# A fused memory attention and feed-forward kernel: padded token rows, keys loaded first, and small matmuls issued in fixed bundles

## The chip, the cores and the metric

The kernel runs on one core of a Trainium2 chip. The metric is the device time of one execution in microseconds (us); the median of three runs is used. TensorE does the matmuls, VectorE and ScalarE the elementwise work, GpSimd small copies, and SyncE issues all DMA transfers.

## What is computed

Eight batches of 576 tokens, eight heads of 64, 32 memory slots per head, then a feed-forward layer of 2048 on the 512 joined columns:

```python
a = phi - np.max(phi, axis=2, keepdims=True)          # over the tokens
a = np.exp(a); a = a / (np.sum(a, axis=2, keepdims=True) + 1e-09)
k_m = np.einsum('bhsm,bhsd->bhmd', a, k)              # 32 x 64 per head
v_m = np.einsum('bhsm,bhsd->bhmd', a, v)
scores = scale * np.matmul(q, k_m.transpose(0, 1, 3, 2))
attn = softmax(scores)                                # over 32 slots
x = np.matmul(attn, v_m)                              # heads joined: 4608 x 512
h = x @ w_in                                          # 512 x 2048
sp = np.maximum(h, 0.0) + np.log1p(np.exp(-np.abs(h)))
out = (h * erf(sp)) @ w_out                           # 2048 x 512
```

The kernel never forms x. It multiplies v_m with w_in once per batch (called "value products" here, `vw`) and multiplies attn with that.

## The kernel before

The weights arrive as 64-bit words and are decoded to float32 on the chip (`decode`: per block of 1 MB, three passes on VectorE and two on ScalarE). Most operands are then split into a high and a low part in float32r, and a product is made of three such matmuls; the first four steps of the first layer and the first sixteen of the second use plain float32 instead, which TensorE runs as two passes (two rows in the trace for one matmul in the program).

A step is one block of 128 hidden columns for the 576 tokens of one batch: sixteen steps to a batch, 128 in all. For a step `ffn1` (L681) makes h in two halves of 288 tokens, VectorE copies it from PSUM (L696), ScalarE runs softplus (L704) and erf (L709) for four steps at a time because each of the two needs its own table, VectorE forms and splits g, and `ffn2` (L754) multiplies by w_out into four PSUM tiles `pso`, one for each 128 tokens. The last 64 tokens of two batches are collected and multiplied together (`psr`).

For each batch four small kinds of TensorE work come ahead of its steps:
- sums (L540): k_m and v_m, by `one_memory`, for two groups of four heads one after the other. Stationary is a block of phi (128 tokens x 32), moving are K and V of a head side by side (128 columns). Tokens lie in chunks of 128, 128, 128, 128 and 64. 20 program matmuls for a group, 4 of them at a time on four column strips of TensorE.
- two transposes that put k_m and v_m (`kvk`, L557) into the layout that the next two kinds want.
- scores (L583, tiles `q`, `km`): q times k_m for 288 tokens, twice per batch (`attention`). Their softmax is ten steps on VectorE and two on ScalarE; its exponential may run only where a group of four softplus or erf ends.
- value products (L583, tiles `w_in`, `vm`): four per batch from the second batch on, with 512 columns.

Sums use TensorE in strips of 32 columns and 128 rows (64 for the last chunk), scores and value products in strips of 32 columns and 64 rows; everything else uses the whole array. A stretch of such small matmuls between two whole-array matmuls is called a visit below.

The order is made by `Plan`: each operation is recorded with an engine, a cost, a rank (100 times the step at which it is wanted), what it reads and writes and which buffers it needs; `order()` runs through a model of the engines' time and writes one fixed program order for each engine. Among what is ready TensorE takes the lowest rank; once in a visit it goes on with other small work that is ready. PSUM has four tiles `ps`, shared by h, all small work and `psr`. While TensorE has nothing in the head, `fill` puts matmuls on zeros there (`idle`, L365). All loads go through SyncE in that order: `load_kv` and `load_phi` take two DMAs each (512 tokens and the last 64), `load_weight` 1 MB, `load_q` 576 KB. The head's list is `FIRST`.

Of the kernel before, what the change touches and what calls it, by code (L numbers as in the profile page):

```python
# [28 lines left out]
SCRATCH = 1024  # L29

# [39 lines left out]
class Plan:  # L70
# [5 lines left out]
    SWITCH = 92.0  # L76
    RELOAD = 100.0
# [160 lines left out]
def tile_memory_attention_then_erf_softplus_ffn(  # L238
# [13 lines left out]
    H = 2 * kv.shape[1]  # L252
    D = 64
# [12 lines left out]
    SC = [(c * P, min(P, S - c * P)) for c in range((S + P - 1) // P)]  # L266
    RAW = 4
# [10 lines left out]
        for n, b, kw in (  # L278
# [9 lines left out]
            ("ot", 2, {}),  # L288
# [6 lines left out]
    room.update({"g_hi": 3, "g_lo": 3, "raw": RAW, "ot": 2, "ps": 4, "sc": 2, "dk": 1, "phiT": 2})  # L295
    room.update({f"pso{d}": 1 for d in range(NT)})
    for n in ("pmx", "psm", "prs"):
# [10 lines left out]
        "ot": ("ot", [P, DM], F32),  # L308
# [18 lines left out]
    def mm(n, exact):  # L327
        return 2 * (2 * n / 2.4 + 2.5) if exact else n / 2.4 + 11.7
# [10 lines left out]
    zeros = const.tile([P, 512], BF16, name="zeros")  # L339
# [12 lines left out]
    def split(rank, hi, lo, src, n, get_hi, get_lo, get_src, psum=False):  # L352
        op(ACT, on_act(n, psum), rank, [src], [hi],
           lambda: nc.scalar.activation(get_hi(), get_src(), AF.Identity))  # L354
        op(DVE, on_dve(n), rank, [src, hi], [lo],
           lambda: nc.vector.tensor_tensor(  # L356
               out=get_lo(), in0=get_src(), in1=get_hi().bitcast(F32), op=ALU.subtract))
# [3 lines left out]
    def fill(n):  # L361
        if n and not idle:
            idle.append(pools["po"].tile([P, DM], F32, name="idle", tag="pso0"))
        for _ in range(n):
            nc.tensor.matmul(out=idle[0], lhsT=zeros[:, :P], rhs=zeros, start=True, stop=True)  # L365


    def load(rank, key, nbytes, emit):
        op(SP, 60, rank, [], [key], emit, nbytes=nbytes)

    def load_weight(rank, name, c):
        key = tile_("wo", "w", name, c, shape=[P, NP_ * 256], dtype=I64, pool="wo")

        def emit():
            t = get(key)
            if name == "in":
                nc.sync.dma_start(
                    out=t.rearrange("p (r f) -> p r f", r=NP_),
                    in_=w_in[:, :, c * 256 : (c + 1) * 256],
# [6 lines left out]
        load(rank, key, P * 8192, emit)  # L386

    def load_phiT(rank, b, g):
        key = tile_("phiT", "phiT", b, g)
        load(rank, key, P * S * 4,  # L390
             lambda: nc.sync.dma_start(out=get(key), in_=phiT[b, g * P : (g + 1) * P, :]))

    def load_tokens(rank, key, src, n_bytes, view):
        n = S // P
        load(rank, (key, "whole"), S // P * P * n_bytes, lambda: nc.sync.dma_start(
            out=view()[:, :n], in_=src[: n * P].rearrange("(p c) e -> p c e", c=n)))
        load(rank + 0.001, (key, "last"), SC[-1][1] * n_bytes, lambda: nc.sync.dma_start(
            out=view()[: SC[-1][1], n], in_=src[n * P :]))

    def load_phi(rank, b):  # L400
        key = tile_("raw", "phi", b, shape=[P, len(SC), H * M], pool="raw")
        load_tokens(rank, key, phi[b], H * M * 4, lambda: get(key))

    def load_kv(rank, b, p, tag="raw"):
        key = tile_(tag, "kv", b, p, shape=[P, len(SC), 2, 2, D], pool=tag)
        load_tokens(rank, key, kv[b, p], 4 * D * 4,
                    lambda: get(key).rearrange("p c x h d -> p c (x h d)"))

    def load_q(rank, u, tag="raw"):
        key = tile_(tag, "q", u, shape=[P, NP_, U], pool=tag)  # L410
        b, hf = divmod(u, 2)
        load(rank, key, P * NP_ * U * 4, lambda: nc.sync.dma_start(
# [6 lines left out]
    def words(key):  # L419
        v = get(key).bitcast(I32).rearrange("p (n two) -> p n two", two=2)  # L420
        return v[:, :, 0], v[:, :, 1]

    def decode(rank, name, c):
        key = ("w", name, c)
        lo, hi = (key, "lo"), (key, "hi")

        def clamp():
            hf = words(key)[1].bitcast(F32)
# [4 lines left out]
        def low():  # L433
            v = words(key)[0]
            nc.scalar.activation(v, v.bitcast(U32), AF.Identity, scale=LOW)  # L435

        def rebias():
            hf = words(key)[1].bitcast(F32)
            nc.scalar.activation(hf, hf, AF.Identity, scale=REBIAS)  # L439

        def merge():
            v, w = words(key)
# [4 lines left out]
        if name == "in":  # L447
            dst = ("w_in", c)
        elif c < NPR - 1:
# [4 lines left out]
        def sign():  # L454
            v, w = words(key)
            if name == "in":
                to = w_in_sb[c // 2][:, :, c % 2 * 256 : (c % 2 + 1) * 256]
# [489 lines left out]
```

## Time and profile before

| | |
|---|---|
| median of three runs | 731.49 us (730.93 to 731.76) |
| the profiled execution | 729.75 us, span of its instructions 728.0 us |
| TensorE busy | 720.0 us (99%), 4816 matmuls |
| VectorE, ScalarE, GpSimd busy | 521.0 us (72%), 449.9 us (62%), 98.7 us (14%) |
| chain that ended last | TensorE 87%, DMA 6%, ScalarE 4% |
| granted TensorE clock | 0.999 of full speed (the 2.4 GHz level) |

Matmuls are pipelined: the length that a row gives for one is longer than the distance to the next, so the pace of TensorE is read from the distance between starts. TensorE also counts as busy while it multiplies zeros in the head. Page section 2 shows VectorE and ScalarE nearly full in the second to the seventh of forty slices and at five to eight tenths later.

### The profile page before, as it was taken

What the parts mean: (1) busy time and instruction counts of PE and PEld (TensorE: products, weight loads), DVE (VectorE), ACT (ScalarE), POOL (GpSimd) and SP (SyncE); (2) the same over time, 40 slices, a digit from 0 to 9 for tenths busy, and PEclk for the clock granted to TensorE, in tenths of its full rate; (3) what the DMA queues carried; (4) which work ended last, traced back from release to release, by engine and by line L of the source; (5) the groups of instructions that cost most, each with busy time, mean ns of one, the idle gap of its engine ahead of it and who ended that gap; (6) DMA issues with size and microseconds to landing.
All of it is one profiled execution on the core that took longest, in us unless ns stands there. A gap on an engine that the chain in (4) does not pass through costs nothing.

```text
span 728.0 us, 12307 instructions
## 1 busy us (share of the span) xinstructions
PE 720.0 (99%) x4816; PEld 553.8 (76%) x4816; DVE 521.0 (72%) x963; ACT 449.9 (62%) x708; POOL 98.7 (14%) x246
## 2 busy tenths in 40 slices
PE   9999999999999999999999999999999999999997
PEld 4456555578887888888788887888878788888885
DVE  3899999689677685877755587777854587666631
ACT  5799999875747666594644556474754266454611
POOL 0011001120111111111111011111111111111110
PEclk9999999999999999999999999999999999999999
DMA  9996332421503115111310214211210100010002
GB/s 321 391 389 227 100 149 82 161 100 43 173 24 108 42 39 178 35 59 34 107 57 1 91 48 127 70 59 33 66 33 1 59 15 0 1 45 15 1 1 72
DMA packets 30393, 64.75 MB, mean 89 GB/s; under 512 B 2688, under 2 KB 13440, under 8 KB 29312
## 3 DMA queue, kind: packets, MB, share of 16 engines
q1 hardware_dynamic: 30336, 63.97, 26.1%
q8 instruction: 38, 0.62, 0.4%
q14 instruction: 19, 0.16, 0.1%
HBM read 54.53 MB, written 9.44 MB: 88 GB/s over the span
## 4 chain that ended last, share of the span: by engine, by line
PE 87%; DMA 6%; ACT 4%; DVE 1%; SPq 1%; issue 1%
PE pso L754 48%; PE psh L681 26%; PE psr L754 6%; PE psa L583 5%; DMA w<-w_in 4%; PE psa L540 2%; DMA kv<-kv 2%; ACT w L439 1%; ACT w L435 1%; ACT e L709 0%; ACT L709 0%; PE psa L557 0%; ACT e L704 0%; DVE w L443 0%; ACT vw_hi L354 0%
## 5 line engine op out<-in xcount | busy, mean ns | idle before, releaser
L754 PE MATMUL pso<-wo,g_hi 128*128 128x512 f32 x896 | 280.8, 395 | 0.0
L704 ACT ACTIVATE e<-h 128x576 f32<-128x576 f32 x128 | 88.0, 687 | 171.5 <-DVE h L696 170.9
L754 PEld LDWEIGHTS pso<-wo,g_hi 128*128 128x128 f32 x896 | 160.0, 188 | 31.8 <-issue 6.3
L754 PE MATMUL pso<-wo,g_lo 128*128 128x512 f32 x448 | 176.1, 393 | 0.0
L696 DVE COPY h<-psh 128x288 f32<-128x288 f32 x239 | 107.8, 452 | 42.8 <-PE psh L681 41.2
L681 PE MATMUL psh<-at_hi,vw_hi 128*128 128x288 f32 x496 | 113.7, 310 | 0.0
L681 PE MATMUL psh<-at_hi,vw_lo 128*128 128x288 f32 x496 | 106.0, 295 | 0.3 <-DVE vw_lo L356 0.3
L681 PE MATMUL psh<-at_lo,vw_hi 128*128 128x288 f32 x496 | 106.1, 295 | 0.0
L681 PEld LDWEIGHTS psh<-at_hi,vw_hi 128*128 128x128 f32 x496 | 84.5, 188 | 27.8 <-issue 8.2
L735 POOL CAST rest<-g_hi 128x64 fp32r<-128x64 f32 x112 | 51.1, 457 | 391.3 <-DVE g_hi L730 385.5
L728 DVE TENSOR_TENSOR e<-e,h 128x576 f32<-128x576 f32 x112 | 82.7, 751 | 26.5 <-ACT e L709 26.4
L754 PEld LDWEIGHTS pso<-wo,g_lo 128*128 128x128 f32 x448 | 84.1, 188 | 19.2
L730 DVE CAST g_hi<-e 128x576 fp32r<-128x576 f32 x112 | 50.7, 457 | 63.1 <-PE pso L754 51.1
L731 DVE TENSOR_TENSOR g_lo<-e,g_hi 128x576 fp32r<-128x576 f32 x112 | 86.3, 771 | 4.4
L709 ACT ACTIVATE e<-e 128x576 f32<-128x576 f32 x128 | 80.3, 675 | 0.4
L681 PEld LDWEIGHTS psh<-at_hi,vw_lo 128*128 128x128 f32 x496 | 79.8, 188 | 0.7 <-DVE vw_lo L356 0.5
L681 PEld LDWEIGHTS psh<-at_lo,vw_hi 128*128 128x128 f32 x496 | 79.1, 188 | 0.0
L735 POOL CAST rest<-g_lo 128x64 fp32r<-128x64 f32 x112 | 37.8, 338 | 110.8 <-DVE g_lo L731 103.7
L754 PE MATMUL pso<-w,g 128*128 128x512 f32 x112 | 52.5, 599 | 0.0
L754 PE MATMUL psr<-wo,rest 128*128 128x512 f32 x192 | 49.0, 390 | 0.0
L354 ACT ACTIVATE vw_hi<-psa 128x512 fp32r<-128x512 f32 (+1 forms) x68 | 34.9, 556 | 19.6 <-PE psa L583 19.5
L356 DVE TENSOR_TENSOR vw_lo<-psa,vw_hi 128x512 fp32r<-128x512 f32 (+1 forms) x68 | 42.0, 632 | 6.5 <-ACT vw_hi L354 6.3
(82 smaller groups left out, 716.0 us busy)
## 6 DMA issues: line engine op xcount, KB each, us to landing
kv<-kv SPq DMA_DIRECT2D x32, 512.0 KB, 4.2
q<-qT SPq DMA_DIRECT2D x16, 576.0 KB, 5.0
w<-w_in SPq DMA_DIRECT2D x8, 1024.0 KB, 11.6
w<-w_out SPq DMA_DIRECT2D x8, 1024.0 KB, 11.2
out<-ot SPq DMA_DIRECT2D x32, 256.0 KB, 2.0
phiT<-phiT SPq DMA_DIRECT2D x16, 288.0 KB, 2.9
phi<-phi SPq DMA_DIRECT2D x8, 512.0 KB, 5.7
kv<-kv SPq DMA_DIRECT2D x32, 64.0 KB, 4.2
```

The source lines that it names most:

```text
L354: lambda: nc.scalar.activation(get_hi(), get_src(), AF.Identity))
L356: lambda: nc.vector.tensor_tensor(out=get_lo(), in0=get_src(), in1=get_hi().bitcast(F32), op=ALU.subtract))
L583: nc.tensor.matmul(out=get(ps[par])[p * M : (p + 1) * M, :], lhsT=w()[rows, p, :], rhs=x()[rows, p, :], start=True, stop=True,)
L681: nc.tensor.matmul(out=get(ps), lhsT=x[:, g, k % 4 * P : (k % 4 + 1) * P], rhs=y[:, g, :], start=(n + g == 0), stop=(n == len(parts) - 1 a ...
L696: lambda: nc.vector.tensor_copy(out=keep(), in_=get(ps)),
L704: last[:] = [op(ACT, on_act(S), rank, [("h", i)], [e], lambda: nc.scalar.activation(get(e), get(("h", i)), AF.Softplus), kind="softplus", ...
L709: last[:] = [op(ACT, on_act(S), rank, [e], [e], lambda: nc.scalar.activation(get(e), get(e), AF.Erf), kind="erf", edge=edge, after=last)]
L728: op(DVE, on_dve(S), rank, [e, h], [e], lambda: nc.vector.tensor_tensor(out=get(e), in0=get(e), in1=get(h), op=ALU.mult))
L730: op(DVE, on_dve(S, 1), rank, [e], [hi], lambda: nc.vector.tensor_copy(out=get(hi), in_=get(e)))
L731: op(DVE, on_dve(S), rank, [e, hi], [lo], lambda: nc.vector.tensor_tensor(out=get(lo), in0=get(e), in1=get(hi).bitcast(F32), op=ALU.subtract))
L735: lambda x=x, y=y: nc.gpsimd.tensor_copy(out=rest[:, k, x, cols], in_=get(y)[:, NT * P :]))
L754: nc.tensor.matmul(out=o, lhsT=y, rhs=z, start=(start and n == 0), stop=(stop and n == len(parts) - 1))
```

## The change

- K and V come as separate arrays, and all token tables are padded on the host to five chunks of 116 rows (the last 112) in 128 partitions, so that each load is one DMA of 640 KB and every chunk takes more than 64 rows. `Plan`'s costs for a switch of strips and for a 512-column matmul are raised.
- The first batch: the loads come as phiT, K, first half of q, the first block of w_in, V, second half of q. phi itself isn't loaded: the exponential of phiT is transposed instead. Its K memories are made first and its first scores go ahead of V (`EARLY`).
- Sums have 64 moving columns instead of 128, since K and V are apart: 80 program matmuls per batch where there were 40, five chunks each.
- From the second batch on one call makes the sums of both groups (`TOGETHER`); from the third batch on `bundle` joins small work into single operations: sums with the third value product of the batch before, the first scores with its fourth, the second scores with the first value product of the batch itself.
- The rest's low part is made on GpSimd for the first batch (`rest_split` is gone), `ot` tiles live in the slots of `phiT`, and ScalarE copies the final results alone.

```diff
+ROW = 116
-    SWITCH = 92.0
-    RELOAD = 100.0
+    SWITCH = 98.0
+    RELOAD = 170.0
...
-    RAW = 4
+    ROWS = [min(ROW, S - c * ROW) for c in range(NC)]
+    RAW = 5
...
+    def together(rank, *pieces):
+        for x in pieces:
+            next(x)
+        reads, writes, holds, emits, cost = [], [], [], [], 0.0
+        for x in pieces:
+            c, r, w, k, emit = next(x)
+            cost, reads, writes, holds = cost + c, reads + r, writes + w, holds + k
+            emits.append(emit)
+        op(PE, cost, rank, reads, writes, lambda: [f() for f in emits], kind="small", holds=holds)
+        for x in pieces:
+            next(x, None)
...
         def sums():
-            for c, (s0, ln) in enumerate(SC):
-                for j in range(4):
-                    h = 4 * g + j
-                    nc.tensor.matmul(
-                        out=get(ps)[M * j : M * (j + 1), 0, :],
-                        lhsT=get(a)[:ln, c, h * M : (h + 1) * M],
-                        rhs=get(("kv", b, h // 2))[:ln, c, :, h % 2, :],
...
+            for n, g in enumerate(gs):
+                for y, x in enumerate(xs):
+                    for c, ln in enumerate(ROWS):
+                        for j in range(4):
+                            h = 4 * g + j
+                            nc.tensor.matmul(
+                                out=get(ps)[M * j : M * (j + 1), n, y * D : (y + 1) * D],
+                                lhsT=get(a)[:ln, c, h * M : (h + 1) * M],
+                                rhs=get(("kv", b, x, g))[:ln, c, j * D : (j + 1) * D],
...
-    FIRST = ["phiT0", "phiT1", "phi", "kv0", "kv1", "in0", "kv2", "kv3", "q0", "q1", "in1", "out0"]
+    FIRST = ["phiT0", "phiT1", "k0", "k1", "q0", "in0", "v0", "v1", "q1", "in1", "out0"]
...
-        n = o - 12 if b == 1 else max(o - 21, NK - 2)
+        n = o - 8 if b == 1 else max(o - 18, NK - 2)
...
-            n = o - (8 if b == 1 else 11) + 4 * x
+            n = o - 8 + 4 * x if b == 1 else o - 7 + 3 * x
             when(n, load_q, at(n - 4), 2 * b + x)
-            when(n, attention, at(n), at(n + 1), 2 * b + x)
-        for p in range(4):
-            n = o - 3 + 4 * p
-            when(n, vw, at(n), b, 2 * p, 2, False)
+        PARTS = [(o - 8, [(attention, 2 * b)]), (o - 4, [(attention, 2 * b + 1)]), (o - 3, [(vw, b, 0)])]
+        if b > 1:
+            PARTS = [
+                (o - 11, [(one_memory, b, TOGETHER[0]), (vw, b - 1, 8)]),
+                (o - 7, [(attention, 2 * b), (vw, b - 1, 12)]),
+                (o - 4, [(attention, 2 * b + 1), (vw, b, 0)]),
+            ]
+        PARTS.append((o + 1, [(vw, b, 4)]))
+        if b == B - 1:
+            PARTS += [(o + 5, [(vw, b, 8)]), (o + 9, [(vw, b, 12)])]
```

What this does to the order of the instructions, at three places. First TensorE's sums for the last batch. Before, the first group of heads follows a value product:

```order
L754 MATMUL pso<-wo,g_hi 128x512 x2
L754 MATMUL pso<-wo,g_lo 128x512
L583 MATMUL psa<-w_in_103,vm_101 32x512 x8
L540 MATMUL psa<-kv,phi 32x128 x20
L681 MATMUL psh<-at_hi,vw_hi 128x288 x2
L681 MATMUL psh<-at_lo,vw_hi 128x288 x2
```

The second group's twenty stand twenty-four rows further on, in a visit of their own. In the changed kernel, for the same batch:

```order
L796 MATMUL pso<-wo,g_lo 128x512
L796 MATMUL psr<-wo,rest 128x512 x6
L585 MATMUL psa<-kv,phi 32x64 x80
L637 MATMUL psa<-w_in_102,vm_98 32x512 x8
L796 MATMUL pso<-wo,g_hi 128x512 x2
L796 MATMUL pso<-wo,g_lo 128x512
```

Both groups, K and V apart, now stand in one visit, and a value product follows the sums instead of leading them. Second, TensorE's first scores of the last batch. Before they stand alone:

```order
L754 MATMUL pso<-wo,g_hi 128x512 x2
L754 MATMUL pso<-wo,g_lo 128x512
L583 MATMUL psa<-q,km_100 32x288 x8
L754 MATMUL pso<-wo,g_hi 128x512 x2
L754 MATMUL pso<-wo,g_lo 128x512
```

In the changed kernel:

```order
L796 MATMUL pso<-wo,g_hi 128x512 x2
L796 MATMUL pso<-wo,g_lo 128x512
L637 MATMUL psa<-q,km_97 32x288 x8
L637 MATMUL psa<-w_in_103,vm_98 32x512 x8
L796 MATMUL pso<-wo,g_hi 128x512 x2
L796 MATMUL pso<-wo,g_lo 128x512
```

The fourth value product of the seventh batch stands behind them in the same visit. Over the whole program there are 51 visits before and 40 in the changed kernel; behind the visit that holds the last value product of the first batch there are 38 and 29. Third, TensorE's start without the matmuls on zeros, whose rows are left out of both (112 in all before, 78 now). Before:

```order
L501 MATMUL psa<-ident,bias 128x128 x2
...
L540 MATMUL psa<-kv,phi 32x128 x20
...
L557 MATMUL psa<-ident,kvk 128x128 x2
...
L540 MATMUL psa<-kv,phi 32x128 x20
...
L557 MATMUL psa<-ident,kvk 128x128 x2
...
L583 MATMUL psa<-q,km_99 32x288 x16
...
L583 MATMUL psa<-w_in_103,vm_101 32x256 x8
...
L681 MATMUL psh<-at,vw_hi 128x288 x8
```

In the changed kernel:

```order
L557 MATMUL psa<-ident,phiT 112x128
...
L585 MATMUL psa<-kv,phi 32x64 x40
...
L607 MATMUL psa<-ident,kvk 128x128 x2
...
L637 MATMUL psa<-q,km_96 32x288 x8
...
L585 MATMUL psa<-kv,phi 32x64 x40
L637 MATMUL psa<-q,km_96 32x288 x8
L607 MATMUL psa<-ident,kvk 128x128 x2
...
L637 MATMUL psa<-w_in_100,vm_98 32x256 x8
...
L737 MATMUL psh<-at,vw_hi 128x288 x4
...
L637 MATMUL psa<-w_in_100,vm_98 32x256 x8
```

The first scores stand ahead of V's sums, the second behind them, and the first four matmuls of `ffn1` (two steps, first half of the tokens) no longer wait for the second scores.

## Rows read from the trace of the kernel before

**Rows 1.** By stretch: us, each engine's busy us (instructions), clock, DMA share, GB/s
```profile
0.00:30.00 30.00, 28.38 (x222) 12.56 (x223) 16.87 (x34) 16.96 (x34) 0.70 (x6) 1.00 0.98 353
30.00:50.00 20.00, 19.44 (x129) 11.69 (x128) 19.39 (x29) 18.46 (x30) 1.50 (x2) 1.00 1.04 380
...
200.00:300.00 100.00, 100.00 (x693) 81.30 (x692) 72.56 (x146) 63.78 (x99) 15.27 (x38) 1.00 0.25 78
```

**Rows 2.** TensorE in order of time, lone visit: start, length, operation, count
```profile
607.83 0.62 PE L754 MATMUL pso<-wo,g_hi 128*128 128x512 f32 x2
608.28 0.40 PE L754 MATMUL pso<-wo,g_lo 128*128 128x512 f32 x1
608.61 1.09 PE L583 MATMUL psa<-w_in,vm 64*32 64x512 f32 x16
609.63 0.53 PE L681 MATMUL psh<-at_hi,vw_hi 128*128 128x288 f32 x2
610.00 0.42 PE L681 MATMUL psh<-at_lo,vw_hi 128*128 128x288 f32 x2
610.26 0.43 PE L681 MATMUL psh<-at_hi,vw_lo 128*128 128x288 f32 x2
```

**Rows 3.** The same view, value products followed by scores
```profile
499.19 1.09 PE L583 MATMUL psa<-w_in,vm 64*32 64x512 f32 x16
500.07 0.69 PE L583 MATMUL psa<-q,km 64*32 64x288 f32 x16
500.69 0.74 PE L754 MATMUL pso<-wo,g_hi 128*128 128x512 f32 x2
```

**Rows 4.** The same view, value products followed by sums
```profile
518.47 1.09 PE L583 MATMUL psa<-w_in,vm 64*32 64x512 f32 x16
519.49 1.43 PE L540 MATMUL psa<-kv,phi 128*32 128x128 f32 x40
520.85 0.53 PE L681 MATMUL psh<-at_hi,vw_hi 128*128 128x288 f32 x2
```

**Rows 5.** The same view, sums alone
```profile
527.90 1.43 PE L540 MATMUL psa<-kv,phi 128*32 128x128 f32 x40
529.27 0.73 PE L754 MATMUL pso<-wo,g_hi 128*128 128x512 f32 x2
```

**Rows 6.** Stretches of those sums: matmuls (PE) and weight loads (PEld) under way
```profile
527.90:527.96 0.06, 0.06 (x4) 0.06 (x8) 1.00 0.00 0
527.90:528.03 0.13, 0.13 (x4) 0.13 (x8) 1.00 0.00 0
...
527.90:528.72 0.82, 0.82 (x32) 0.81 (x32) 1.00 0.00 0
```

**Rows 7.** TensorE's order of time in the head
```profile
20.19 0.84 PE L583 MATMUL psa<-q,km 64*32 64x288 f32 x16 [0.29 <-DMA q<-qT]
...
22.09 7.73 PE L365 MATMUL idle<-zeros 128*128 128x512 bf16 x35
29.66 4.04 PE L681 MATMUL psh<-at,vw_hi 128*128 128x288 f32 x16
```

**Rows 8.** VectorE's and ScalarE's order of time in the head
```profile
12.82 0.70 DVE L429 TENSOR_SCALAR w<-w 128x1024 f32<-128x1024 f32 x1 [3.99 <-DMA w<-w_in]
...
28.26 1.43 DVE L650 STREAM_TRANSPOSE at<-sc 128x576 f32<-128x576 f32 x2
...
31.31 1.22 DVE L465 SCALAR_TENSOR_TENSOR w_in<-w 128x1024 int32<-128x1024 int32 x1
...
27.96 1.17 ACT L435 ACTIVATE w<-w 128x1024 int32<-128x1024 uint32 x1 [0.58 <-DMA w<-w_in]
```

**Rows 9.** TensorE's order of time at the third batch's sums
```profile
129.16 1.42 PE L540 MATMUL psa<-kv,phi 128*32 128x128 f32 x36 [0.58 <-DMA kv<-kv]
```

**Rows 10.** Groups by line and shape: busy us, mean ns, idle before
```profile
L704 ACT ACT_TABLE_LOAD x33 | 42.3, 1283 | 0.6
...
L521 ACT ACTIVATE phiT<-phiT,pmx 128x576 f32<-128x576 f32 x16 | 12.3, 771 | 0.1
```

More of the change, by code (lines that the diff above doesn't have):

```diff
@@ L265, in tile_memory_attention_then_erf_softplus_ffn @@
     REST = S - NT * P
-    SC = [(c * P, min(P, S - c * P)) for c in range((S + P - 1) // P)]
-    RAW = 4
+    NC = phi.shape[2]
+    ROWS = [min(ROW, S - c * ROW) for c in range(NC)]
+    assert NC == -(-S // ROW) and D < ROWS[-1]
+    RAW = 5
     HB, EB = 5, 5
@@ L364, in fill, with load, load_weight @@
         for _ in range(n):
[L365 to L372, printed above, removed]
+            nc.tensor.matmul(
+                out=idle[0].rearrange("p (n c) -> p n c", c=P), lhsT=zeros,
+                rhs=zeros.unsqueeze(1).to_broadcast([P, DM // P, P]), start=True, stop=True,
+            )
+    def load(rank, nbytes, keys, emit):
+        op(SP, 60, rank, [], keys, emit, nbytes=nbytes)
+    def load_weight(rank, name, c, x=None):
+        n = 256 if x is None else P
+        key = tile_("wo", "w", name, c, x, shape=[P, NP_ * 256], dtype=I64, pool="wo")
         def emit():
@@ new lines, in memories @@
+        if not b:
+            tile_("raw", *a, shape=[P, NC, H * M], pool="raw")
+            n = NC - 1
+            for g in range(NG):
+                numbers_of(rank, b, g, range(n), tile_("ps", "psa", "a", g, shape=[P, n, P], pool="ps"), 0)
+            last = tile_("ps", "psa", "a", NG, shape=[P, NG, P], pool="ps")
+            for g in range(NG):
+                numbers_of(rank, b, g, range(n, NC), last, g)
+        for turn_n, part in enumerate(parts):
+            together(rank_2 + turn_n * 0.01, one_memory(rank_2 + turn_n * 0.01, b, part))
@@ L576, in heads @@
-    def heads(rank, reads, w, x, n, holds, *key):
-        ps = [tile_("ps", "psa", *key, par, shape=[P, n], pool="ps") for par in range(2)]
-        def emit():
-            for p in range(NP_):
-                for par in range(2):
-                    rows = slice(par * D, (par + 1) * D)
-                    nc.tensor.matmul(
-                        out=get(ps[par])[p * M : (p + 1) * M, :],
-                        lhsT=w()[rows, p, :],
-                        rhs=x()[rows, p, :],
-                        start=True,
-                        stop=True,
-                    )
-        op(PE, 4 * n / 2.4, rank, reads, ps, emit, kind="small", holds=holds)
-        return ps
@@ new lines, in heads, with of_heads @@
+    def heads(n, *key):
+        return [tile_("ps", "psa", *key, par, shape=[P, n], pool="ps") for par in range(2)]
+    def of_heads(ps, w, x):
+        for p in range(NP_):
+            for par in range(2):
+                rows = slice(par * D, (par + 1) * D)
+                nc.tensor.matmul(
+                    out=get(ps[par])[p * M : (p + 1) * M, :],
+                    lhsT=w[rows, p, :],
+                    rhs=x[rows, p, :],
+                    start=True,
+                    stop=True,
+                )
@@ L670, in ffn1 @@
         ws = [("vw_hi", b, k // 4)] if exact else [("vw_hi", b, k // 4), ("vw_lo", b, k // 4)]
-        part = [(k // 2 % 2, par) for par in range(2)] if b == 0 else [(0, par) for par in range(2)]
+        part = [(k % 4, par) for par in range(2)]
         h = ("h", i)
@@ L852, in tile_memory_attention_then_erf_softplus_ffn @@
             when(2 * c - 3, decode, at(2 * c - 3), "in", c)
-            when(2 * c - 1, vw, at(2 * c - 1.5), 0, c, 1, 2 * c < FR1)
-        when(2 * c, decode, at(second[2 * c] - 3.5), "out", c)
+            n = at(2 * c - 1.5)
+            when(2 * c - 1, lambda n=n, c=c: together(n, vw(n, 0, 2 * c, 2, 2 * c < FR1)))
+        when(2 * c, decode, at(second[2 * c] - 2.5), "out", c)
         n = second[16 + 2 * c] - 5 - c if 2 * c < FR2 else second[2 * c] - 2
```

311 lines of the change are left out of this document (163 added, 148 removed).

## The prediction

> **What bounds the kernel now.** I read the engines' busy time by stretch first, since the page's 99% for TensorE hides what it is busy with. Between 200 and 300 us TensorE is busy for all 100 us and VectorE for 73, ScalarE for 64; in the first 50 us VectorE and ScalarE fill up to 19.4 and 18.5 of 20 us while TensorE does matmuls on zeros for a good part of its busy time [rows 1, 7]. So there are two regimes. From about 90 us on, TensorE alone sets the pace, and each 0.1 us less on it is 0.1 us less at the end. Before, the loads, the decoding of weights and the first softmax do, and what TensorE saves there is worth nothing.
>
> For the second regime the useful view is TensorE's order of time, read by the distance of starts. In the steady stretch a 512-column matmul follows the last after 0.227 us (two take 0.45) and a 288-column one after 0.13 us [rows 2]. Now a visit of small matmuls: the last whole-array matmul takes 0.33 us until the value product starts, 0.10 more than its pace; the value product takes 1.02 us until the next whole-array matmul, but 0.88 when scores follow, which use the same strips [rows 2, 3], so leaving costs 0.14; and the first two matmuls behind take 0.37 instead of 0.26 us, 0.11 more [rows 2]. **A visit costs 0.35 us beside its work.** No row of that regime shows TensorE waiting for another engine.
>
> For the first regime: the second scores wait for the second half of q until 20.19 us, then come both softmaxes interleaved on VectorE up to 29.7 us (the last transposition starts at 28.26 and takes 1.43), and only then, at 29.66, the first product; thirty-five matmuls on zeros fill the time [rows 7, 8].
>
> **The change, part by part.**
>
> Visits. Behind the last value product of the first batch the program order has 38 visits before and 29 now. Nine of them at 0.35 us are 3.2 us, all in the stretch where TensorE is the bound. Visits ahead of that are in the first regime and I count them as nothing.
>
> Changes of strips within a visit. Where sums follow a value product, the value product again takes 1.02 instead of 0.88 us [rows 3, 4], so a change from 64-row to 128-row strips costs the same 0.14 us. Sums alone take 1.37 us [rows 5]; eight of their ten rounds of four have started after 0.82 us, some 0.11 us each [rows 6]; ten rounds are 1.1, leaving is 0.14, and the remaining 0.13 us is the change to the last chunk, which has 64 rows. The new chunks all take more than 64 rows, so that goes: twelve groups in the third to the eighth batch, 1.6 us. Value products ahead of sums go five times and behind sums come six times, +0.1 us. Together −1.5 us.
>
> The sums themselves. A batch had twenty rounds (two groups, five chunks, two passes) of 128 columns at 0.11 us, 2.2 us. It now has forty rounds of 64 columns, and no row shows one of these. Lower end: a round costs by its columns, 0.055 us, and the sum stays at 2.2 us. Upper end: a round takes 0.11 us whatever it streams, and a batch costs 4.4 us, 2.2 more. I take a value near the lower end, +0.1 us per batch, because the rows show nothing else in a round that takes long: within 0.06 us four matmuls and eight weight loads are under way, and for the next 0.07 us no matmul starts [rows 6], so loads are out early and the round waits for its columns. Six batches: +0.6 us; the range keeps +13.
>
> A wait. At the third batch's sums TensorE sits idle for 0.58 us until a K and V load lands [rows 9]. In the new order these sums stand some five steps later, and the load is one DMA instead of two. −0.6 us.
>
> The head. Ahead of the second half of q before stand 5632 KB, landed at 20.19 us; ahead of the first block of w_in 3328 KB with it, landed at 12.82 [rows 7, 8]. That is some 260 KB per us. The first half of q now has 2432 KB with it, so it lands at about 9.4 us, and K before that. One visit of sums, the copies and the scores bring this to about 12 us, a softmax to 21 or 22 (the two together took 9.5 us, and a decode runs beside the new one), and V's part, 4736 KB, lands near 17 and is ready for the value product by 21. So the first half of the first two steps can start at about 22 us instead of 29.66, some 2 us of matmuls (both halves of two steps took 4.04 [rows 7]). The second half has its q at 5312 KB, near 19 us, and is ready near 29, as before. The second block of w_in, whose last decoding pass ended at 32.5 us behind both softmaxes [rows 8], should be decoded some 4 us earlier, as VectorE has half the softmax behind it. What comes later is bound by VectorE and ScalarE, which are both full between 30 and 50 us [rows 1], and these inherit the earlier start but not all of it: the third block of w_in, which ScalarE awaited until 27.96 us [rows 8], lands less than 1 us earlier. The work there shrinks a little (two copies per batch less on ScalarE, the splitting of the rest gone to GpSimd, which is busy 15% of the time [rows 1]). Between 0 and 8 us; I take −4.
>
> The second softmax. The second scores of a batch now stand only some two steps ahead of the products that need them, where they had some seven. Their exponential goes between softplus and erf, behind a table load of 1.28 us, and in every batch but the last two exponentials of 0.77 us and the exponential of phi follow it before the split of the result [rows 10]; VectorE's passes are queued in order behind the copies of h. TensorE's next halves of h are queued behind this wait. Counted along these rows it is ready about when TensorE comes to it; from 0 to 2 us late per batch. I take +0.5 us over all.
>
> At nothing: GpSimd's added subtractions (sixteen, off every chain in the head), ScalarE's wider final copies (behind matmuls but for the last), the larger loads (DMA moves 78 GB/s in the steady stretch against 380 in the head [rows 1]).
>
> **Sum:** −3.2 −1.5 +0.6 −0.6 −4 +0.5 = −8.2 us. On the profiled execution's 729.75 us this gives 721.6; the median of the runs is 731.49, 1.7 us above, and on that I forecast **723.3 us**.
>
> **Rivals.**
>
> Short matmuls that aren't short. If TensorE can't start matmuls with their weight loads faster than the 0.11 us for four that the rows show over a whole group [rows 6], each batch's sums take 2.1 us more than in my sum, 12.6 us for six batches: 723.3 + 12.6 = **736 us, slower**. It turns the sign from 1.4 us per batch on, a round of 0.09 us. For it: no stretch shows a sustained pace above this one. Against: the starts come in bursts of four in far less.
> The Trainium skill (TensorE: Matmul & The Clock Gate, "Wait — 56ns, not 53.3ns?") says that matmuls never start closer than about 25 ns to each other, however few columns they have. By that page, as an estimate, 160 passes per batch take 4.0 us, and the time would be near 734 us. The trace does not bear the rule out for the four strips of one round, which start within 0.06 us [rows 6], and no run here shows it for a long row of short ones.
>
> The head gives nothing. If decoding by VectorE and ScalarE sets the time at which TensorE is full, and both work through the same amount, the earlier first product only lengthens the wait behind it: 723.3 + 4 = **727.3 us**. For it: both are full from 30 us on [rows 1]. Against: they have 13 us free in the first 30 [rows 1].
>
> The second softmax comes late. At 2 us for each of six batches, 723.3 + 12 − 0.5 = **734.8 us**. For it: the order leaves it no slack. Against: the kernel before also had one softmax of every other batch end just ahead of its products, and TensorE did not wait.
>
> **How the numbers follow.** My forecast has 0.53 (717 to 729 us), the short matmuls 0.16, the empty head 0.16, the late softmax 0.15. The range from 716 to 735 leaves out the upper part of the short matmuls and of the late softmax and what lies below a head gain of 8 us, 0.2 together. About 0.2% (1.5 us) is what a measurement of this kernel can tell from no change. Faster by more: the forecast, the empty head and the milder part of the other two, 0.75; within: 0.08; slower: 0.17.
>
> **What would show it.** Right: the sums of a batch take some 2.3 us in one visit, TensorE's first product starts near 22 us, 40 visits, no idle TensorE behind 100 us, and VectorE and ScalarE run out of decoding some 4 us earlier. Wrong: rounds of sums at 0.11 us; a gap on TensorE ahead of the second half of a batch's first step, released by the split of the softmax; the first products early but the same time at which the last w_in block is decoded.

## The result and the profile after

| | before | changed |
|---|---|---|
| median of the runs beside each other | 731.62 us (730.93 to 731.95) | 723.20 us (721.90 to 725.49) |
| the profiled execution | 729.75 us, span 728.0 us | 725.49 us, span 723.7 us |
| visits of small matmuls on TensorE | 51 | 40 |
| VectorE, ScalarE busy | 521.0 us, 449.9 us | 516.4 us, 433.6 us |

The ratio is 0.989 (0.986 to 0.992): **8.4 us faster, where 8.2 us, 723.3 us, was forecast**. The profiled execution of the changed kernel is the slowest of its four, 2.3 us above the median; why, the rows at 90 us below show. Its stretches, as in [rows 1] (us, each engine's busy us with instructions, granted clock, DMA share, GB/s):

```profile
0.00:30.00 30.00, 26.42 (x306) 12.34 (x306) 18.15 (x37) 15.89 (x29) 0.70 (x6) 1.00 0.96 352
30.00:50.00 20.00, 19.16 (x119) 12.83 (x118) 19.78 (x30) 19.91 (x30) 3.48 (x5) 1.00 1.03 407
200.00:300.00 100.00, 100.00 (x757) 83.99 (x756) 69.59 (x134) 53.07 (x78) 13.93 (x39) 1.00 0.20 65
```

The steady stretch is TensorE's alone, as before. There a lone visit has the same price as in [rows 2]. TensorE's order of time (start, length, operation, count):

```profile
621.96 0.39 PE L796 MATMUL pso<-wo,g_lo 128*128 128x512 f32 x1
622.28 1.09 PE L637 MATMUL psa<-w_in,vm 64*32 64x512 f32 x16
623.30 0.53 PE L737 MATMUL psh<-at_hi,vw_hi 128*128 128x288 f32 x2
623.66 0.42 PE L737 MATMUL psh<-at_lo,vw_hi 128*128 128x288 f32 x2
```

0.32 us to the value product, 1.02 until the next whole-array matmul, 0.36 for the first two. Now a bundle, sums with a value product, where [rows 4, 5] had two visits:

```profile
222.50 2.45 PE L585 MATMUL psa<-kv,phi 116*32 116x64 f32 x160
224.88 1.09 PE L637 MATMUL psa<-w_in,vm 64*32 64x512 f32 x16
225.90 0.74 PE L796 MATMUL pso<-wo,g_hi 128*128 128x512 f32 x2
```

A batch's sums take 2.38 us to the value product. Their rounds, as in [rows 6], show that a round of four takes 0.055 us: nine passes have started after 0.12 us, and all 160 in 2.24 us.

```profile
222.49:222.61 0.12, 0.12 (x9) 1.00 0.00 0
222.49:224.73 2.24, 2.24 (x160) 1.00 0.18 27
```

Two things are new. In the third batch's visit, and in the fifth batch's at 304.99, **TensorE stops in the middle of the value product with nothing to wait for** ("issue"):

```profile
149.58 2.46 PE L585 MATMUL psa<-kv,phi 116*32 116x64 f32 x160
151.97 0.61 PE L637 MATMUL psa<-w_in,vm 64*32 64x512 f32 x1
153.37 1.09 PE L637 MATMUL psa<-w_in,vm 64*32 64x512 f32 x15 [0.79 <-issue]
```

From 149.58 to the next whole-array matmul this visit takes 4.81 us, the one at 304.99 takes 4.72, and the other four 3.40: 2.7 us for both stops. (The wait that the row names is shorter, since the modelled end of the matmul ahead covers a part.)

The second new thing is in the head. The first product starts at 23.87 us, 5.8 us ahead of [rows 7], but the second batch's scores wait for q:

```profile
23.87 2.18 PE L737 MATMUL psh<-at,vw_hi 128*128 128x288 f32 x8 [0.19 <-DVE at L706]
...
88.03 0.43 PE L737 MATMUL psh<-at_hi,vw_lo 128*128 128x288 f32 x2
90.17 0.84 PE L637 MATMUL psa<-q,km 64*32 64x288 f32 x16 [1.71 <-DMA q<-qT]
90.93 1.67 PE L796 MATMUL pso<-w,g 128*128 128x512 f32 x2
...
92.88 0.68 PE L737 MATMUL psh<-at_lo,vw_hi 128*128 128x288 f32 x2
93.36 0.68 PE L737 MATMUL psh<-at_hi,vw_lo 128*128 128x288 f32 x2
```

Both halves of q were issued from 82.89 us on, as the second batch's sums let go of the five "raw" tiles (the buffers that phi, K, V and q share), and moved beside phi, K and V of the third batch. The stretches behind the wait show a granted clock down to 0.50, the 1.2 GHz level. There matmuls start at nearly twice the distance: 0.24 us for 288 columns at 92.88, as against 0.13.

```profile
88.00:90.00 2.00, 0.45 (x4) 0.21 (x2) 1.48 (x4) 1.99 (x4) 0.78 (x2) 1.00 1.07 395
90.00:92.00 2.00, 1.83 (x19) 0.97 (x19) 0.93 (x3) 1.97 (x3) 0.00 (x0) 0.84 1.02 410
92.00:94.00 2.00, 2.00 (x11) 1.32 (x10) 1.22 (x2) 0.61 (x1) 0.56 (x2) 0.50 1.01 330
94.00:96.00 2.00, 2.00 (x19) 0.60 (x19) 1.79 (x3) 0.46 (x1) 0.06 (x1) 0.80 0.21 87
```

To say where time went, I take from all TensorE records the time beside products: time passed, less what the products of the first and second layer, the rests, the scores and the value products take at their own pace (0.229 us for a 512-column pass, 0.132 for 288 columns, as the rows above; a row of the plain float32 products takes nearly twice that, 0.25 us for 288 columns in [rows 7]). These are the same in every kernel here. Only differences between kernels are used, taken before rounding. Stops are counted from 100 us on.

| profiled execution | us beside products to 100 us | from 100 to 705 us | of it in stops | VectorE busy to 40 us | median of runs |
|---|---|---|---|---|---|
| before | 41.9 | 34.7 | 0 | 26.3 | 731.6 |
| changed | 41.0 | 31.6 | 2.7 | 28.0 | 723.2 |
| changed, repeated | 37.8 | 31.7 | 2.5 | 28.6 | 722.3 |
| K and V side by side | 39.2 | 28.5 | 0 | | 720.4 |
| bundles apart | 39.2 | 35.1 | 0 | | 728.2 |
| chunks of 128 | 37.8 | 34.7 | 1.1 | | 726.7 |
| head as before | 43.8 | 33.2 | 3.9 | 23.0 | 730.3 |
| q early, sums in one visit | 44.7 | 33.8 | 4.5 | 20.3 | 731.9 |
| keys first, q late | 40.1 | 32.6 | 3.7 | 26.3 | 725.6 |

### The profile page after: what moved, and what is told of

The parts are those of the page before. It is cut to its first block, busy times and chain, and to the rows that moved or that the text cites. A ratio compares the mean times of both kernels' runs of the same rounds, so it can differ in the third digit from the quotient of the medians.

```text
span 723.7 us, 13374 instructions
## 1 busy us (share of the span) xinstructions
PE 711.9 (98%) x5430; PEld 557.7 (77%) x5430; DVE 516.4 (71%) x950; ACT 433.6 (60%) x642; POOL 103.3 (14%) x262
## 4 chain that ended last, share of the span: by engine, by line
PE 89%; ACT 6%; DMA 3%; SPq 1%; issue 0%; DVE 0%
PE pso L796 48%; PE psh L737 26%; PE psr L796 6%; PE psa L637 6%; DMA q<-qT 3%; PE psa L585 2%; ACT w L442 1%; ACT w L438 1%; ACT e L760 1%; SPq L409 1%; ACT e L765 1%; ACT L760 1%; ACT h L753 0%; PE idle L368 0%; PE psa L607 0%
## 5 line engine op out<-in xcount | busy, mean ns | idle before, releaser
L737 PEld LDWEIGHTS psh<-at_hi,vw_hi 128*128 128x128 f32 x496 | 86.5, 189 | 22.1 <-issue 8.2
L792 POOL CAST rest<-g_lo 128x64 fp32r<-128x64 f32 x112 | 34.0, 304 | 90.6 <-DVE g_lo L788 86.4
```

The costliest lines, as they stand in the source:

```text
L737: nc.tensor.matmul(out=get(ps), lhsT=x[:, g, k % 4 * P : (k % 4 + 1) * P], rhs=y[:, g, :], start=(n + g == 0), stop=(n == len(parts) - 1 a ...
L792: lambda x=x, y=y: nc.gpsimd.tensor_copy(out=rest[:, k, x, cols], in_=get(y)[:, NT * P :]))
```

## Experiments

**The changed kernel again.** 

> The changed kernel again, unaltered. Its first profile shows two things that the prediction did not have: the second batch's first scores wait 1.7 us for q at 90 us, with TensorE's granted clock below 1.0 until 96 us, and two of the six visits with sums and a value product take 4.8 and 4.7 us instead of 3.4, with a break inside the value product. Theory: both belong to the program. Then this profile has a wait for q of 1 to 2 us near 90 us, a clock below 1.0 behind it, and a break of over 0.5 us in at least one of the six visits; the median is 723.2 us within 1 us. Rival: they belong to that one execution. Then the wait or the breaks are missing, and the median can lie some 2 us lower.

Measured: 722.34 us (722.24 to 723.30). The stops came again in the same two visits, 1.2 and 1.3 us. The wait for q was there too, but 1.0 us, and the clock stayed up. TensorE's waits from 60 to 100 us (in total, times, longest):

```profile
PE psa L637 <- DMA q<-qT: 1.0, 1, 1.0
```

So the stops belong to the program; the wait for q belongs to it too, but its length differs by execution, and the first profiled one had a long one with the lower clock behind it. Up to 100 us the two executions differ by 3.1 us (41.0 and 37.8).

### The stops

**Half as many instructions.**

```diff
-  for y, x in enumerate(xs):                         # K, then V: 64 columns each
-      out=get(ps)[M*j : M*(j+1), n, y*D : (y+1)*D], rhs=get(("kv", b, x, g))[:ln, c, j*D : (j+1)*D]
+  # second batch on: K and V of a head beside each other, 128 columns
+      out=get(ps)[M*j : M*(j+1), n, : 2*D], rhs=get(("kv", b, j//2, g))[:ln, c, j%2*P : (j%2+1)*P]
```

> From the second batch on K and V lie side by side in a tile, and a sum is one matmul of 128 columns instead of two of 64: 40 matmuls (80 passes) per batch in place of 80 (160), the same sums, the same loads, the same order. Theory 1, TensorE runs out of instructions behind a long row of short ones: with half of them the six visits take 3.4 us each, no break above 0.3 us, and the time falls by what the breaks cost, 2.7 us in the first profile, to 720.5 to 722 us. Theory 2, the breaks come from something else that happens at the same time (the loads): they stay, in one or two visits, and the time stays at 723.2 us within 0.7. Theory 3, rounds of 64 columns cost more than half a round of 128: every visit is shorter, by 0.2 us or more, also those without a break. The prediction priced the sums at 0.1 us per batch above those of 128 columns.

Measured: 720.38 us (719.79 to 721.61), 2.0 below the repeat. No stop in any visit. The visit that stopped before:

```profile
147.62 2.43 PE L586 MATMUL psa<-kv,phi 116*32 116x128 f32 x80
149.98 1.09 PE L646 MATMUL psa<-w_in,vm 64*32 64x512 f32 x16
151.00 0.73 PE L805 MATMUL pso<-wo,g_hi 128*128 128x512 f32 x2
```

The sums take 2.36 us here and 2.33 in the five others (2.38 in the changed kernel), so short columns cost 0.05 us per batch. Theory 1, and theory 3 only in that small amount.

**Twice as many.**

```diff
-  for y, x in enumerate(xs):
+  for y, x in list(enumerate(xs)) * (2 if b > 1 else 1):
```

> From the third batch on each sum is computed twice in a row into the same place: 160 matmuls (320 passes) per batch, and the same result. The row of short instructions is twice as long. By the measured 2.24 us per batch the sums alone add 13.4 us to 722.3. Theory 1, TensorE runs out of instructions because a long row of short ones outruns their supply: all six visits now have breaks, of 1.2 us or more in sum each, most of them inside the sums, and the time is 741 to 750 us. Theory 2, the breaks come from a load or another event that happens at two of the six visits: two breaks as before, 735.7 us within 1.

Measured: 762.96 us (759.17 to 766.72). All six visits stop, most of them twice, and the second stops are longer than I had thought:

```profile
145.81 2.49 PE L585 MATMUL psa<-kv,phi 116*32 116x64 f32 x161
149.17 2.00 PE L585 MATMUL psa<-kv,phi 116*32 116x64 f32 x128 [0.87 <-issue]
155.09 1.08 PE L585 MATMUL psa<-kv,phi 116*32 116x64 f32 x31 [3.92 <-issue]
```

Between the two stops lie 128 matmuls with their weight loads, 256 instructions. The stops make 25 us in sum. Theory 1; its size was missed.

Numbering TensorE's records in the order in which they start gives the rule. Counted are weight loads, matmuls and the hundred or so instructions with which TensorE waits for semaphores. The list has the number of records ahead of each stop from 12 us on in which TensorE stood still with nothing to wait for, over 0.6 us from start to start, in kernels of this study, some of which follow below:

```
changed, repeated        2497, 5057                    (both alike)
second batch earlier     1217, 2497, 5057
head as before           449, 2497, 3777, 9153
q early, one visit       449, 2497, 3777, 9153
keys first, q late       2497, 5057, 9153
sums twice               2497, 2753, 4033, 4289, 5825, 7361, 7617, 9153, 10689, 10945
54 more                  2497, 3777, 9153
150 more                 1729, 7873
```

Divided by 256, each leaves 193. The queue that carries instructions brings one packet of 16 KB for 256 records: 38 packets for 9758 records before (38.1 times 256), 43 for 10954 in the changed kernel (42.8), 50 for 12874 with the sums twice (50.3). And in each case such a packet had ended 1.2 to 1.6 us before TensorE went on; here the one that ran from 150.74 to 152.04 us, with TensorE going on at 153.37 (the stretch from 150.6 to 152.2: packets, MB, share):

```profile
q8 instruction: 1, 0.02, 5.1%
```

**Moving the block ends.** If blocks of 256 are the cause, other instructions far ahead must move the stops to other visits.

```diff
+  if quarters[0]:                 # 9 (54 more) or 25 (150 more) of the matmuls on zeros
+      quarters[0] -= 1
+      for x in range(DM // P):
+          nc.tensor.matmul(out=idle[0][:, x*P : (x+1)*P], lhsT=zeros, rhs=zeros, start=True, stop=True)
+      continue
```

> The changed kernel with the first nine matmuls on zeros in the head each cut into four of 128 columns, which puts 54 more instructions (27 weight loads, 27 matmuls) ahead of everything else; sums, loads and order are untouched. Numbered along TensorE's records, all breaks so far began at instruction 2496 or a multiple of 256 behind it, in just those visits in whose row of 352 short instructions two such places lie: the first and third of six. Theory: TensorE's instructions come in blocks of 256, and a block that is worked off in 2.3 us ends before the next is there. Moved on by 54, two such places lie in the first, second, third and sixth visit: four breaks of 0.9 to 1.4 us, and 722.3 + 2.4 = 724.7 us, if the head is not disturbed. Rival, the breaks go with the loads of K, V and q at those times: they stay in the first and third visit, 722.3 us within 1.

> The same with the first twenty-five matmuls on zeros cut into four: 150 more instructions ahead. Theory, blocks of 256: two block ends lie in the fifth visit alone (near 470 us); the breaks in the first and third visit are gone, one of 0.9 to 1.4 us comes in the fifth, and the time is 722.3 - 1.3 = 721 us, if the head is not disturbed. Rival, loads: breaks in the first and third visit, 722.3 us within 1.

Measured: with 54 more, stops in the first, second and sixth visit (0.7, 1.3, 1.3 us); the third, where I expected a fourth, had none. With 150 more, none of the six but the fifth:

```profile
471.14 2.33 PE L591 MATMUL psa<-kv,phi 116*32 116x64 f32 x151
474.97 0.36 PE L591 MATMUL psa<-kv,phi 116*32 116x64 f32 x9 [1.49 <-issue]
475.25 1.09 PE L643 MATMUL psa<-w_in,vm 64*32 64x512 f32 x16
```

So the place in the instruction stream decides, and the loads do not. The missing stop fits with instructions being read ahead: there the first block end lies only 24 instructions into the visit, and the next block may have been on its way before the visit began. That is argued, not shown: visits of other kernels with 12 to 16 had no stop either, but here the first visit, with 13, did. The times, 725.77 and 723.64 us, don't follow the stops alone: both heads came out 1.8 us later than in the repeat (39.7 against 37.8 at 100 us), with a wait for q of 2.5 us in the first and a stop of 1.1 us at 89.02 us (record 1729) in the second.

The Trainium skill (Runtime: NRT & Kernel Launch, "Instruction fetch mechanics") says that an engine's instructions are refilled in blocks of 256 while the block at hand is executed, and that crossing a block's end is mostly hidden. The trace agrees on the block, and shows where the hiding ends: a block of these short ones is worked off in some 2 us (TensorE passes the 256 instructions ahead of the stop at 151.97 in 2.0 us), and the next one is usable later than that. Up to 100 us slower blocks ended in stops too: those at records 449, 1217 and 1729 stand behind blocks that took 2.3 to 4.9 us. The DMA engines were nearly full there (share 0.94 to 1.07); whether that is why was not tried.

### Visits and strips

**Bundles apart.**

```diff
-  together(rank, *(f(...) for f, *args in fs))
+  for n, (f, *args) in enumerate(fs):
+      together(rank + 50 * n, f(...))
-  if e == PE and small and any(...):
+  if e == PE and False and small and any(...):
```

> The changed kernel with its bundles taken apart: from the third batch on each of the sums, scores and value products is an operation of its own, the second of a pair due half a step later, and the planner no longer prefers a small operation behind a small one. The program order has 14 more visits than in the changed kernel. Theory 1, a visit costs 0.35 us: 4.9 us more than the repeat's 722.3 us, 727.2 us, if the two breaks of 1.2 us stay (now behind the sums, in whole-array matmuls), and 724.7 us if sums that stand alone no longer run TensorE out of instructions. Theory 2, visits were never worth their price: 722.3 us within 0.7, or 719.8 without the breaks.

Measured: 728.18 us (727.18 to 728.29), 5.8 above the repeat. The trace has 57 visits, 17 more and not 14. Of the stops, 0.3 us behind the fifth batch's sums are left. The only wait of TensorE from 100 to 718 us is one for a store:

```profile
PE pso L796 <- ACT ot L839: 0.6, 1, 0.6
```

17 visits at 0.35 us less 2.5 us of stops are 3.4 us, and the time beside products from 100 us on rose by 3.4 (35.1 against 31.7), 0.6 of it this wait. Six of the 17 part sums from a value product; there the leaving takes the place of a change of strips, and a visit costs only the 0.10 on entry and the 0.11 behind it. Counted so, with the wait and the stop, 6 x 0.21 + 11 x 0.35 - 2.5 + 0.6 + 0.3 is 3.5 us, and the price of a visit holds. Of the rest of the 5.8 us, 1.4 lies ahead of 100 us, where the program is nearly the same, and 1.0 is not explained.

**Chunks of 128.**

```diff
-ROW = 116
+ROW = 128
```

> Tokens in chunks of 128 rows again, four and a last one of 64, in place of five of 116 and 112; the sums are in the new order, so the last chunk comes four times in a batch's sums. Prediction's term: a change of strips costs 0.13 us. Into the last chunk four times and out of it three, and none on the way to the value product, which uses 64-row strips too: 0.8 us per batch, six batches, 4.7 us, 727 us. If only one of the two directions costs: 0.4 us per batch, 724.6 us. Rival, the strips were nothing and the 0.13 us was something else: 722.3 us within 0.7. The breaks in two of the six visits can get shorter, as the instructions are spread over more time.

Measured: 726.66 us (725.47 to 727.05), 4.3 above the repeat. A visit without a stop went from 3.40 to 4.18 us; its end shows the last chunk of 64 rows:

```profile
389.24 3.33 PE L585 MATMUL psa<-kv,phi 128*32 128x64 f32 x156
392.34 0.65 PE L637 MATMUL psa<-w_in,vm 64*32 64x512 f32 x4
392.39 0.24 PE L585 MATMUL psa<-kv,phi 64*32 64x64 f32 x4
```

0.78 us per batch against the 0.8 expected, 4.7 in six, less 1.5 us by which the stops shrank: 3.2, and the table has 3.0 (the profiled executions differ by 3.1, the medians by 4.3). Both directions of a change cost 0.13 us. The starts in this visit show it without the sum: a round of four takes 0.056 us in chunks of 128 rows, as in those of 116; the first two rounds behind a change take 0.17 and 0.08 us, into the last chunk and out of it alike, 0.13 to 0.14 us more for both together.

### The wait for q

**Second batch earlier.**

```diff
-  n = o - 8 if b == 1 else max(o - 18, NK - 2)
+  n = o - 12 if b == 1 else max(o - 18, NK - 2)
```

> The second batch's loads of phi, K and V, its first softmax and its sums are due four steps earlier (steps 4 and 7 instead of 8 and 11), as in the kernel before; nothing else is edited. The sums then let go of their tiles before q is wanted. Theory 1, the head's gain was given back at the wait for q: no wait for q above 0.3 us, the granted clock stays at 1.0 from 80 to 100 us, TensorE's lost time at 100 us is 3 to 4 us less, and the time is 719 to 720.5 us. Theory 2, VectorE and ScalarE set the pace until 100 us, and the wait only stood where they were late anyway: the wait goes, others come, and the time is 723.2 us within 1 us.

Measured: 723.94 us (723.59 to 725.23). TensorE waits for nothing from 60 to 100 us, and yet it has lost 39.6 us at 100 us against 37.8. The moved sums brought a stop of their own, though, ahead of that stretch (record 1217):

```profile
58.14 0.53 PE L737 MATMUL psh<-at_hi,vw_hi 128*128 128x288 f32 x2 [0.98 <-issue]
```

From start to start it is 1.27 us, 1.1 more than the pace. Even without it TensorE would have lost some 38.4 us, and not the 3 to 4 us less of theory 1. That fits theory 2, by which the wait stood in time that VectorE and ScalarE would have taken anyway; with the stop in it, the run does not measure what the wait is worth.

**Keys first in the second batch too**, on top of K and V side by side from the third:

```diff
-  memories(..., TOGETHER if b == 1 else [])
+  memories(..., EARLY if b == 1 else [])
```

> K and V side by side from the third batch on, as in the run before of 720.4 us, and keys first in the second batch as in the first: its K sums are a visit of their own and let go of two tiles, which q takes, before V is summed. Two loads for the third batch then no longer run beside q. Theory 1, the wait for q near 90 us and the lower clock behind it cost what they show, 1 to 3 us: no wait for q above 0.4 us, clock 1.0 between 88 and 98 us, less 0.4 us for the added visit, 718 to 719.7 us, with less scatter. Theory 2, VectorE and ScalarE set the pace up to 100 us, and the wait for q only stands where they would be waited for: 720.4 us within 0.7.

Measured: 719.74 us (719.32 to 721.00). The wait for q is 0.4 us and the clock 1.0. This is the fastest kernel of the study (0.983 of before, 0.982 to 0.985), but 0.6 us from side by side alone, with overlapping runs: it doesn't tell the theories apart.

### The head

**Taken back, whole and by halves.** The order of loads, and the split of the first batch's sums into K and V:

```diff
-  FIRST = [..., "k0", "k1", "q0", "in0", "v0", "v1", "q1", ...]     # head as before; keys first, q late
+  FIRST = [..., "k0", "k1", "in0", "v0", "v1", "q0", "q1", ...]
-  memories(at(-10), at(-9), 0, EARLY)                               # head as before; q early, one visit
+  memories(at(-10), at(-9), 0, TOGETHER)
```

> The changed kernel with the head's order taken back: K and V of the first batch are both loaded ahead of both halves of q, and their sums are one visit. Bundles, strips and chunks stay. Theory 1, the prediction's term: the first product starts near 29 us instead of 21.9, and all of it is 4 us, 727 us. Theory 2, the wait for q near 90 us takes what the head gave: the first product is as late, but at 100 us TensorE has lost 1 to 2.5 us more than in the changed kernel, and the time is 724 to 725.5 us. Theory 3, the head is worth nothing: 723.2 us within 0.7.

> The changed kernel with only one half of the head's order taken back: loads stay (the first half of q ahead of V), but the first batch's sums of K and V are one visit that waits for V. With both halves taken back the time was 730.3 us, against 722.3. Theory 1, what counts is when the first softmax can start, and it needs both the keys' own visit and q ahead of V: the first scores come near 20 us instead of 12.6, the first product near 30, and the time is 728 to 730 us. Theory 2, each half is worth a part: 725.5 to 727 us.

> The other half taken back: the keys' sums stay a visit of their own, but both halves of q are loaded behind V, as before. Theory 1: the first scores wait for q until some 20 to 22 us, the first product comes at 29 to 32 us, and the time is 728 to 730.3 us, as in the run with both halves taken back. Theory 2, each half is worth a part: 725.5 to 727 us.

Measured: 730.32 us with both taken back, 731.88 with q early but one visit, and 725.63 with the keys' own visit but q late. All my numbers for the whole were too low (727 at most, 730.3 came), those for q early with one visit too (730 at most); keys first with q late fits theory 2. The first products came at 32.00, 36.04 and 28.73 us, against 23.28 in the repeat. So the keys' visit with a late q starts its products 5.5 us later than the changed kernel and loses 3.3 us, 1.2 of it in more stops (three against two).

The other two changed more than was meant. With K and V in one visit the first batch too has 160 passes in a row, and TensorE stops behind them (record 449). Head as before, TensorE and then VectorE, which waits for the scores:

```profile
18.05 0.80 PE L607 MATMUL psa<-ident,kvk 128*128 128x128 f32 x4
21.39 0.82 PE L368 MATMUL idle<-zeros 128*128 128x512 bf16 x3 [2.54 <-issue]
22.14 1.20 PE L637 MATMUL psa<-q,km 64*32 64x288 f32 x32
```

```profile
22.94 1.58 DVE L685 STREAM_TRANSPOSE sc<-psa 128x288 f32<-128x288 f32 x4 [4.66 <-PE psa L637]
```

q early, one visit:

```profile
22.33 0.82 PE L368 MATMUL idle<-zeros 128*128 128x512 bf16 x3 [3.37 <-issue]
22.98 0.98 PE L607 MATMUL psa<-ident,kvk 128*128 128x128 f32 x4
```

In the first, the scores' inputs were there by about 20 us, so the stop delays them by some 2 us; in the second, ScalarE had the transposes' input ready at 19.87 us, and the stop delays them by 3.1. By estimate, with these delays and the 1.4 and 2.0 us of further stops behind 100 us taken off in full, some 4.5 us are left of the 8.0 and of the 9.5 us that these kernels lose, and 2.1 of the 3.3. How much of a delay in the head comes through to the end was not tried.

What the four heads do follow is VectorE's busy time in the first 40 us (third engine in a row; repeat, head as before, q early with one visit, keys first with q late):

```profile
0.00:40.00 40.00, 35.98 (x367) 19.44 (x368) 28.59 (x52) 26.44 (x45) 0.70 (x6) 1.00 0.97 368
```

```profile
0.00:40.00 40.00, 36.14 (x355) 18.04 (x356) 23.01 (x43) 23.15 (x37) 0.70 (x6) 1.00 0.97 363
```

```profile
0.00:40.00 40.00, 35.40 (x349) 17.53 (x350) 20.28 (x40) 20.17 (x32) 0.70 (x6) 0.96 0.97 367
```

```profile
0.00:40.00 40.00, 36.13 (x367) 19.59 (x368) 26.33 (x50) 24.83 (x44) 0.70 (x6) 1.00 0.97 366
```

Against the repeat, 2.3, 5.6 and 8.3 us less of it (keys first, as before, one visit) go with 2.3, 6.0 and 6.9 us more beside products at 100 us. From 40 to 90 us VectorE is busy for 46 to 49 of 50 us in all of them, so what it leaves undone early comes back nearly in full. That is a relation over four kernels, not a wait that was removed, and in two of them part of what VectorE left undone is the stop.

## Why the prediction was right, and where it was not

The time was forecast within 0.1 us, but not for quite the reasons given: an unforeseen cost and better terms cancel. That it came so close is luck.

- **Visits, −3.2 us: right.** The entry, the leaving and the first pair are as priced, and the bundles taken apart cost what 17 visits should, within the 0.6 us of a wait and 1.0 us that is not explained. From 100 us on there were ten fewer, not nine.
- **Strips, −1.5 us: right.** 0.13 us per change, shown by the starts in the chunks of 128.
- **Sums, +0.6 us: right, a little less.** 0.05 us per batch instead of 0.1. The first rival, short matmuls that aren't short, is out: a round takes 0.055 us. The Trainium skill's floor of about 25 ns between starts (TensorE: Matmul & The Clock Gate, "Wait — 56ns, not 53.3ns?") does not hold for matmuls on different strips: 160 of them start within 2.24 us, 14 ns apart.
- **The K and V wait, −0.6 us: right.** No such wait behind 100 us.
- **The second softmax, +0.5 us: wrong, nothing.** TensorE waited for no softmax, and the third rival is out.
- These five were −4.2 us together. From 100 us on the time beside products fell by 5.9 us apart from the stops (34.7 to 31.6, and 2.7 of the 31.6 are stops).
- **Missing: +2.7 us for the stops.** The step that failed is the one that priced the short matmuls by columns or by a fixed time each, and put what hides their supply at nothing: the number of instructions had no term. The row that bore on it, 38 packets of instructions, stands on the page of the kernel before.
- **The head, −4 us: near in size, its reason not shown.** Over the eight executions with this head, up to 100 us, TensorE was 0.9 to 4.5 us better off than before, 2.9 us in the mean (41.0, 37.8, 39.2, 39.2, 37.8, 39.7, 39.7 and, with the sums twice, 37.4, against 41.9). I had it follow from the first product, which I put at 22 us (23.87), and let VectorE and ScalarE take half of it. The halves of the head suggest that VectorE's early work counts for more than the first product's start, but a stop of TensorE lies in two of the three kernels that speak for it, so the reason stays open. VectorE's last pass on w_in, where I expected 4 us, ended 7.5 us earlier: 81.79 against 89.33 us. The wait for q, which I didn't foresee, took a part back. The second rival, an empty head, is out: keys first with a late q loses 2.1 us beside its added stops, and taking all of it back costs 8.0 us. That is more than the head's worth: the stop at 21.39 us is in it, and with it that kernel's first product comes 2.3 us later than before's.
- The sum of what was measured in profiled executions, −2.9 −5.9 +2.7, is −6.1 us. The medians differ by 8.4: before's profiled execution was 1.9 us under the median of its runs beside these, and where in it these 1.9 us lie stays open.

## What to carry to other kernels

Count instructions beside columns: from the third batch on, rows of up to some 190 short matmuls and weight loads never stopped here, and rows of 352 did wherever a whole block of 256 lay well inside them. Joining small work into longer bundles can cross that line, and wider matmuls (K and V side by side) undid it and lost nothing. An experiment that joins or moves such rows moves the stops too, so look for them before reading its time. In a head where a vector engine has more work than time, ask what lets it start, and not only when the first product runs. A wait that stands in such a stretch may be worth nothing, so take it away by experiment before counting it.

## What was not expected of the hardware

- TensorE stops at the end of a block of 256 instructions (weight loads, matmuls and waits for semaphores counted) that it has worked off in some 2 us: by 0.4 to 1.7 us at the first in a row, and up to 3.9 us at the second. In the head two such stops left it idle for 2.5 and 3.4 us.
- The granted clock after a wait differs: it fell to 0.50 behind a wait of 1.71 us in the first profiled execution, and stayed at 1.00 behind one of 2.51 us with 54 instructions more:

```profile
88.00:90.00 2.00, 0.00 (x0) 0.00 (x0) 1.27 (x3) 1.99 (x4) 0.32 (x1) 1.00 1.12 386
90.00:92.00 2.00, 1.50 (x19) 0.82 (x19) 0.72 (x3) 1.97 (x3) 0.00 (x0) 1.00 1.03 407
92.00:94.00 2.00, 2.00 (x23) 0.91 (x21) 2.00 (x5) 0.16 (x1) 0.56 (x2) 1.00 1.01 399
```
